# A streaming attention decode on one core: the first load split in 16 and 112 rows, and the semaphores cleared ahead of the last wait

## The chip, the cores and the metric

The kernel runs on one core of a Trainium2 chip. The core has five engines with instruction streams of their own: TensorE (PE in the profile), VectorE (DVE), ScalarE (ACT), GpSimd (POOL) and SyncE (SP), and sixteen DMA engines that move data between the memory (HBM) and the on-chip buffer (SBUF, 128 partitions). The metric is the device time in microseconds (us) of one execution; lower is better. Engines and transfers are kept in order by semaphores: an instruction can wait until a semaphore has reached a value, and an instruction or a transfer adds to one when it is done. A transfer adds 16.

## The reference

Two one-token attention decodes, A and B, with separate inputs, whose outputs are put side by side:

```python
q = (x @ wq).reshape(B, Sq, Hq, Dh)            # x: 1x512, wq: 512x4096, 32 heads of 128
scores = einsum("bhqd,bhkd->bhqk", q, k) * Dh ** -0.5
p = softmax(scores)
o = einsum("bhqk,bhkd->bhqd", p, v)
out = o.reshape(1, 1, 4096) @ wo               # wo: 4096x512
```

A sees the whole cache of 16384 positions, B the last 4096 (a window). Everything is bf16. Each head has its own keys and values, so all of K and V is read once: 128 MiB each for A, 32 MiB each for B, and four weights of 4 MiB. The result has 1024 numbers.

## The kernel before

All large loads are issued by SyncE, one behind the other, and run over all 128 partitions. Three SBUF slots of 8 MiB hold them: slotX and slotY take the key tiles in turn, slotV the values; before the first values arrive, the two halves of slotV hold the weights wq of A and B, and at the end both wo.

There are twenty steps (`steps`), sixteen of A with two heads each and four of B with eight heads each (steps 0, 7, 13 and 19). In each, VectorE multiplies the key tile with the query and adds up along the head's 128 numbers (`scores_prod`, `scores_tree`), TensorE and VectorE find the maximum (`tile_trs`, `tile_max`, `max_all`), ScalarE takes the exponential (`soft`), and TensorE multiplies with the values (`tile_pv`) and folds the result into an accumulator (`tile_fold`). TensorE's part of the loop is a hardware loop.

The order of the loads is written out by hand. Before a first barrier (`tc.close(); tc.compile()`), SyncE issues four loads of 4 MiB without any wait: wq of B (`load_wq`, line 197), the first half of the keys of step 0 (line 181), wq of A, the second half of those keys. ScalarE issues the two small loads of x at the same time. wq goes into slotV by `"(p c) f -> p c f"`: partition p takes four neighbouring rows of the matrix, so 32 KiB in one piece. After that each key load waits until VectorE is done with the slot's earlier tile, and each value load until TensorE is done with slotV. The queue so holds one to two loads ahead of the one that is running.

TensorE starts with the projection of B as soon as its wq is there (line 276), then that of A.

At the end the two wo are loaded, that of B in five pieces (16, 8, 4, 3 and 1 blocks of every partition, line 448), so that little is left to do behind the last piece: sixteen small matmuls (line 595), one copy by VectorE from PSUM into `rows_b` (line 601), and two stores of the result's second half (line 605), one by ScalarE and one by SyncE, that both wait for that copy. The first half of the result was stored by ScalarE before (line 588). All three stores count on one semaphore, `in_out`. GpSimd waits until it has all 48, and then clears all semaphores that the kernel took (`nc.clear_and_free_semaphores(sems)`, line 610): they have to be zero for the next execution.

```python
    wq_in = [None, load_wq(B, wq[1], in_wqB)]
    load_k(0, (0,))
    wq_in[0] = load_wq(A, wq[0], in_wqA)
    load_k(0, (1,))
    tc.close()
    tc.compile()
```

## Time and profile before

| What | Value |
|---|---|
| time, median of 3 runs | 820.95 us (820.79 to 821.01) |
| the profiled execution, its own time | 821.11 us |
| its span, first to last instruction | 819.2 us |
| moved by DMA | 352.40 MB |
| mean rate over the span | 430 GB/s |
| busy: VectorE | 755.7 us (92%) |
| busy: TensorE | 191.5 us (23%) |
| busy: ScalarE | 57.5 us (7%) |
| busy: GpSimd | 3.5 us |

The span is counted from the first to the last instruction of the program; what lies around it, 1.9 us here, is in the execution's time but not in the trace. A core's DMA engines work in packets; a packet of a large load is one partition's piece, 32 or 64 KiB. The chain of waits is followed back from the last instruction and tells what the end waited for. The table of windows gives, for each stretch, the busy time of each engine and then the clock granted to TensorE, the mean share of time in which the sixteen DMA engines were busy, and the rate. Packets are put down there by the time at which they begin, so that in short stretches the share can be over 1.

### The profile page before, as it was taken

To read this page: it belongs to the slowest core of one execution; us is meant where nothing else is said; L and a number is where in the kernel's file an instruction comes from. 1 tells how busy PE (TensorE), PEld (TensorE's weight loads), DVE (VectorE), ACT (ScalarE), POOL (GpSimd) and SP (SyncE) were. 2 spreads that over 40 slices of the span, in tenths; PEclk is the share of its full clock that TensorE was granted. 3 is DMA by queue.
4 is the path that set the end of the run, shared out by engine and by line. 5 is a ranking of instruction groups with operands and counts; after the bars stand their busy time and mean duration, and the time that the engine had idled before them with its cause. 6 is when DMAs were issued, how large, how long until landed. Compare 5 with 4: busy or idle time off the path is not lost. (4 is left out here: it accounts for less than half of the span.)

```text
span 819.2 us, 4049 instructions
## 1 busy us (share of the span) xinstructions
PE 191.5 (23%) x1638; PEld 78.0 (10%) x1638; DVE 755.7 (92%) x264; ACT 57.5 (7%) x165; POOL 3.5 (0%) x15
## 2 busy tenths in 40 slices
PE   3500312213130304030304122131303040303046
PEld 1200101101010101010101011010101010101013
DVE  2899899999999999899999999998999999999992
ACT  0101000001010000100000000010100000000011
POOL 1000000000000000000000000000000000000000
PEclk9765756575665656565656565656656565656567
DMA  9999999999999999999999999999999999999998
GB/s 384 435 435 435 458 413 455 416 454 413 451 419 451 410 432 448 413 458 413 454 416 454 416 454 413 458 413 432 438 454 416 451 416 454 416 434 437 416 432 338
DMA packets 8084, 352.40 MB, mean 430 GB/s; under 512 B 907, under 2 KB 1038, under 8 KB 1294
## 3 DMA queue, kind: packets, MB, share of 16 engines
q1 hardware_dynamic: 8068, 352.33, 99.5%
q8 instruction: 3, 0.05, 0.0%
q14 instruction: 3, 0.02, 0.0%
q10 hardware_dynamic: 10, 0.00, 0.0%
HBM read 352.32 MB, written 0.00 MB: 430 GB/s over the span
## 5 line engine op out<-in xcount | busy, mean ns | idle before, releaser
L306 DVE TENSOR_TENSOR slotX<-slotX,qA 128x16384 bf16<-128x16384 bf16 x18 | 156.3, 8682 | 15.1 <-DMA slotX<-in_A_k_cache_dram 15.1
L315 DVE TENSOR_TENSOR slotY<-slotY 128x8192 bf16<-128x8192 bf16 (+4 forms) x52 | 168.2, 3234 | 1.7
L315 DVE TENSOR_TENSOR slotX<-slotX 128x8192 bf16<-128x8192 bf16 (+4 forms) x44 | 167.0, 3795 | 1.5
L398 PE MATMUL o<-slotV,pm 128*32 128x512 bf16 x1216 | 107.9, 533 | 193.8 <-PEq L165 193.8
L306 DVE TENSOR_TENSOR slotY<-slotY,qA 128x16384 bf16<-128x16384 bf16 x14 | 121.5, 8682 | 8.2 <-DMA slotY<-in_A_k_cache_dram 8.2
L398 PEld LDWEIGHTS o<-slotV,pm 128*32 128x32 bf16 x1216 | 45.1, 128 | 248.8 <-issue 240.7
L391 PE MATMUL sm<-identf,m 128*2 128x128 f32 x20 | 7.4, 372 | 199.5 <-PEq L165 199.5
L306 DVE TENSOR_TENSOR slotY<-slotY,qB 128x16384 bf16<-128x16384 bf16 x6 | 52.1, 8682 | 0.0
L393 PE MATMUL sm<-identf,Mr 2*128 2x2 f32 x20 | 4.7, 233 | 190.2 <-PEq L165 190.2
L354 ACT ACTIVATE bias<-sm 128x1 f32<-128x1 f32 (+1 forms) x20 | 3.4, 171 | 441.8 <-PE sm L393 441.8
L385 ACT COPY osb<-o 128x512 f32<-128x512 f32 x20 | 11.7, 586 | 270.0 <-PE o L398 270.0
L306 DVE TENSOR_TENSOR slotX<-slotX,qB 128x16384 bf16<-128x16384 bf16 x2 | 17.4, 8686 | 12.9 <-ACT qB L282 12.9
L408 PE MATMUL accA<-osb,fwA 128*128 128x512 f32 x38 | 20.8, 630 | 14.8 <-PEq L165 14.8
L322 DVE TENSOR_REDUCE sc<-slotY 128x256 f32<-128x2048 bf16 (+1 forms) x13 | 23.3, 1794 | 0.4
L322 DVE TENSOR_REDUCE sc<-slotX 128x256 f32<-128x2048 bf16 (+1 forms) x11 | 23.0, 2092 | 0.4
L393 PEld LDWEIGHTS sm<-identf,Mr 2*128 2x128 f32 x20 | 3.5, 177 | 196.1 <-issue 196.1
L391 PEld LDWEIGHTS sm<-identf,m 128*2 128x2 f32 x20 | 1.6, 80 | 215.1 <-issue 215.1
L408 PE MATMUL accB<-osb,fwB 128*128 128x512 f32 x40 | 20.5, 594 | 0.5 <-PEq L165 0.5
L367 ACT ACTIVATE pm<-osb,maskA 128x256 bf16<-128x256 bf16 x32 | 14.5, 500 | 0.5
L359 ACT ACTIVATE osb<-sc,bias 128x256 bf16<-128x256 f32 (+1 forms) x24 | 11.3, 470 | 0.6
L276 PE MATMUL t<-slotV,slotY 128*128 128x512 bf16 x32 | 10.0, 488 | 5.0 <-DMA slotV<-in_B_wq_dram 5.0
L276 PE MATMUL t<-slotV,osb 128*128 128x512 bf16 x32 | 8.8, 445 | 9.0 <-DMA slotV<-in_A_wq_dram 9.0
(72 smaller groups left out, 99.4 us busy)
## 6 DMA issues: line engine op xcount, KB each, us to landing
slotV<-in_B_v_cache_dram SPq DMA_DIRECT2D x6, 4096.0 KB, 30.7
slotY<-in_B_k_cache_dram SPq DMA_DIRECT2D x6, 4096.0 KB, 35.3
slotX<-in_B_k_cache_dram SPq DMA_DIRECT2D x2, 4096.0 KB, 30.6
slotX<-in_B_v_cache_dram SPq DMA_DIRECT2D x2, 4096.0 KB, 35.4
slotV<-in_B_wq_dram SPq DMA_DIRECT2D x1, 4096.0 KB, 12.3
slotV<-in_A_wq_dram SPq DMA_DIRECT2D x1, 4096.0 KB, 30.6
slotV<-in_A_wo_dram SPq DMA_DIRECT2D x1, 4096.0 KB, 22.5
slotV<-in_B_wo_dram SPq DMA_DIRECT2D x1, 2048.0 KB, 27.0
```

The lines of the kernel that those rows point to most:

```text
L276: mm = nc.tensor.matmul(qp, lhsT=s.xb[:, j, c, :], rhs=w[:, c, j, g : g + 4, :], start=(k == 0), stop=(k == KC * s.nh - 1),)
L306: return dve.did(nc.vector.tensor_tensor(out=kt, in0=kt, in1=s.q[:, j : j + 1, :].broadcast_to([P, CH, DH]), op=ALU.mult))
L315: t = dve.did(nc.vector.tensor_tensor(out=k[:, :, 0:w], in0=k[:, :, 0:w], in1=k[:, :, w : 2 * w], op=ALU.add))
L322: kfree[T] = dve.did(nc.vector.tensor_reduce(out=sc[:, lo:hi], in_=k[:, :, 0:8], axis=AX.X, op=ALU.add))
L354: t = act.did(nc.scalar.activation(out=bias[:, 0:U], in_=sm[:, P : P + U], func=ACT.Copy))
L359: exped[T] = act.did(nc.scalar.activation(out=p[:, u * n : (u + 1) * n], in_=sc[:, u * n : (u + 1) * n], func=ACT.Exp, scale=inv, bias=bia ...
L367: mm = nc.scalar.activation(out=by_chunk[j], in_=p.rearrange("p (u i c) -> p u i c", u=2, c=4), func=ACT.Copy, scale=s.mask[:, j : j + 1],)
L385: nc.scalar.copy(osb[:, :], o[:, :]).then_inc(to_f, 1)
L391: pe.did(nc.tensor.transpose(sm[0:2, 0:P], m[:, 0:2], identf[:, :]))
L393: pe.did(nc.tensor.transpose(sm[:, P : P + 2], Mr[0:2, :], identf[0:2, 0:2]))
L398: mm = nc.tensor.matmul(o[r0 : r0 + QR, :], lhsT=pm[:, QR * i : QR * (i + 1)], rhs=vf[:, 512 * i : 512 * (i + 1)], start=(i < NG), stop=(i ...
L408: mm = nc.tensor.matmul(a[:, :], lhsT=fw[k][:, :], rhs=osb[:, :], start=False, stop=len(sides) == 1, skip_group_check=True,)
```

## The change

Two places are changed.

The load of B's wq, the first large load of the program, becomes two transfers: partitions 0 to 15, and then partitions 16 to 127. Both count on `in_wqB`, and the projection waits for both (32 in place of 16). All other loads stay as they are; the wq of A keeps one transfer.

At the end a new semaphore, `at_end`, which is not among those cleared, takes the place of the others: VectorE's last copy adds 1 to it, each of the two last stores waits for that and adds 16, GpSimd too waits for the copy alone, clears the semaphores, and adds 1. SyncE waits until `at_end` has 1 + 16 + 16 + 1 = 34 and sets it back to zero. GpSimd's wait for the store of the first half is set right behind that store's issue.

```diff
-    sems = []
+    sems, at_end = [], nc.alloc_semaphore("at_end")
...
-    def load_wq(s, dst, loads):
-        return loads.put(
-            early(nc.sync.dma_start(
-                out=dst.rearrange("p (c f) -> p c f", c=KC), in_=s.wq.rearrange("(p c) f -> p c f", c=KC)
-            ))
-        )
+    def load_wq(s, dst, loads, rows=(P,)):
+        dst, src = dst.rearrange("p (c f) -> p c f", c=KC), s.wq.rearrange("(p c) f -> p c f", c=KC)
+        p0 = 0
+        for n in rows:
+            t = loads.put(early(nc.sync.dma_start(out=dst[p0 : p0 + n, :, :], in_=src[p0 : p0 + n, :, :])))
+            p0 += n
+        return t
...
-    wq_in = [None, load_wq(B, wq[1], in_wqB)]
+    wq_in = [None, load_wq(B, wq[1], in_wqB, (16, P - 16))]
...
-    in_out.put(nc.scalar.dma_start(out=out[0, :, 0:DN], in_=row_a[0:1, :]))
+    pool.need(in_out.put(nc.scalar.dma_start(out=out[0, :, 0:DN], in_=row_a[0:1, :])))
...
-    t = dve.did(nc.vector.tensor_copy(rows_b, last[:, 0:w]))
-    for k, lane in enumerate((act, sp)):
+    nc.vector.tensor_copy(rows_b, last[:, 0:w]).then_inc(at_end, 1)
+    for k, engine in enumerate((nc.scalar, nc.sync)):
         row = QR * (2 * k + 1)
-        lane.need(t)
-        stored = in_out.put(lane.engine.dma_start(
+        engine.wait_ge(at_end, 1)
+        engine.dma_start(
             out=out[0, 0, DN + 2 * k * w : DN + 2 * (k + 1) * w].rearrange("(g f) -> g f", g=2),
             in_=rows_b[row - 1 : row + 1, :],
-        ))
-    pool.need(stored)
+        ).then_inc(at_end, 16)
+    nc.gpsimd.wait_ge(at_end, 1)
     nc.clear_and_free_semaphores(sems)
+    nc.gpsimd.sem_inc(at_end, 1)
+    nc.sync.wait_ge(at_end, 34).then_inc(at_end, -34)
```

## The prediction, made before the result was known

> **What bounds the kernel now.** I read the page first, for the bound:

> ```profile
> span 819.2 us, 4049 instructions
> ...
> DMA  9999999999999999999999999999999999999998
> ...
> DMA packets 8084, 352.40 MB, mean 430 GB/s; under 512 B 907, under 2 KB 1038, under 8 KB 1294
> ...
> q1 hardware_dynamic: 8068, 352.33, 99.5%
> ...
> slotV<-in_B_wq_dram SPq DMA_DIRECT2D x1, 4096.0 KB, 12.3
> ```

> The DMA engines are busy in every slice, SyncE's queue (q1) alone for 99.5% of the span. VectorE's 92% comes second. So the time is: when the stream begins, 352.33 MB at the stream's rate, and what follows the last byte. The packet records of the trace say what the rate is: every DMA engine takes 1.213 us for each 32 KiB piece, 27.0 GB/s, one behind the other with no gap (16 engines give 432 GB/s). It is the same for wq, keys, values and wo. Each 128-row load is 8 pieces to an engine.

> Then the start, in the table of windows (the last two columns are DMA share and GB/s):

> ```profile
> 1.00:1.50 0.50, 0.00 (x0) 0.00 (x0) 0.00 (x0) 0.00 (x0) 0.00 (x0) 1.00 0.00 0
> 1.50:2.00 0.50, 0.00 (x0) 0.00 (x0) 0.00 (x0) 0.00 (x0) 0.00 (x0) 1.00 2.15 524
> 2.00:2.50 0.50, 0.00 (x0) 0.00 (x0) 0.00 (x0) 0.00 (x0) 0.00 (x0) 1.00 1.30 395
> 2.50:3.00 0.50, 0.00 (x0) 0.00 (x0) 0.00 (x0) 0.00 (x0) 0.00 (x0) 1.00 0.36 131
> 3.00:3.50 0.50, 0.00 (x0) 0.00 (x0) 0.00 (x0) 0.00 (x0) 0.00 (x0) 1.00 0.00 0
> 3.50:4.00 0.50, 0.00 (x0) 0.00 (x0) 0.00 (x0) 0.00 (x0) 0.00 (x0) 1.00 1.53 655
> ```

> and in order of time, the issues that go with it:

> ```profile
> 0.74 0.41 SPq L197 DMA_DIRECT2D slotV<-in_B_wq_dram  x1
> 1.20 0.62 SPq L181 DMA_DIRECT2D slotX<-in_B_k_cache_dram  x1
> ```

> The first load is issued at 0.74. Its first sixteen packets, one to an engine, begin between 1.778 and 2.741 (packet records), and nothing new begins until they end, between 3.74 and 4.26, at 3.96 in the mean. They take 1.4 to 2.3 us, 1.9 in the mean, where every later one takes 1.213. From there the stream never stops.

> Last the end, from the chain of waits and the order of time:

> ```profile
> 786.30 30.19 DMA slotV<-in_B_wo_dram
> 816.50 0.04 issue
> 816.54 0.66 PE last L595 x14
> 817.20 0.02 issue
> 817.23 0.29 DVE slotY L601
> ```

> ```profile
> 817.54 0.33 SPq L605 DMA_DIRECT2D out_dram<-slotY  x1
> 817.55 0.26 ACTq L605 DMA_DIRECT2D out_dram<-slotY  x1
> ```

> The last piece of wo is what ends. Behind it stand 0.7 us of matmuls, 0.3 us of copy, and 1.62 us from the stores' issue to the last instruction. The semaphore records split that: the stores' packets move at 818.30, their last increment arrives at 818.833, GpSimd's drain begins at 818.857 (0.10 us), its clearing of the semaphores at 818.986 (0.18 us), and that is the span's end, 819.168.

> **The change part by part.** *The end.* GpSimd's wait, drain and clearing move from behind the stores' landing to behind VectorE's copy, done at about 817.52. Drain, clearing and one increment are 0.10 + 0.03 + 0.18 and some 0.05: done by about 817.95. What hides them is the flight of the stores until 818.833, 0.9 us of cover; were it gone, the 0.31 us would be back. Behind the landing stands SyncE's one wait (semaphore waits in the first barrier are 17 ns long and come 40 to 50 ns after their release). So the last instruction ends near 818.89 in place of 819.17: 0.28 us less. Bounds: 0, if what lies around the span waits for something else, and 0.31, all of drain and clearing. SyncE has nothing queued behind its new wait. GpSimd's added wait for the first half's store (last increment at 815.16) is over 2 us before the copy; nobody waits for GpSimd there. The stores' own waits are the same, on another semaphore: nothing.

> *The start, one issue more.* SyncE issues five transfers ahead of the barrier where it issued four: one more of 0.41 to 0.62 us. The keys' issue slips from 1.20 to about 1.7, still far ahead of its turn at about 12 us. The barrier opens at 3.6 to 4.0 now, behind SyncE's last issue, and would open 0.5 us later; behind it are the constants, the x loads' transposition (now at 7.8, waiting for x) and the projection (now at 13.1, waiting for wq). VectorE's spreading of x ends at 10.9, 2 us ahead of its use: hidden. The next SyncE wait, at 23.1, comes with three loads in flight, so the queue doesn't run dry, and a shift of the stream shifts everything alike.

> *The start, when the stream begins.* A two-row store needs 0.755 us from issue (817.545) to first packet (818.300); the 128-row load needs 1.04 (0.737 to 1.778). Sixteen rows stand near the small one: 0.755 + 0.285 x 14/126 = 0.79, so first packets at about 1.52, 0.25 us earlier. Bounds: 0, since the first packets end together whatever their start, as if all wait for the memory; and 1.2 (0.25 plus the 0.96 us over which engines begin). The engine that lands last at the end isn't the one that began last: increments of wq's load spread over 0.48 us, those of the last wo piece over 1.89, where three engines lag by about 1.6; they fell behind between 80 and 100, 138 and 158, and 544 and 563 us, not at the start.

> [...] No run here shows such a transfer; the trace shows only that 128 partitions get 430 GB/s.

> *The other 112 rows.* Seven pieces to an engine, 7 x 1.213 = 8.49 us, if each engine again has a way of its own. If an engine takes seven neighbouring rows, the groups no longer fall on eights, ways are used by two engines at times: up to 2 x 8.49, so 0 to 8.5 us more. By the nearest row, the 128-row load with no such sharing, I take 0.

> *Sum.* +2.75 at the start, -0.28 at the end: +2.47. The profiled execution's 821.11 (span 819.2 and 1.9 around it) would become 823.58; it stands 0.16 us above the median of 820.95, and against that the forecast is 823.4 us.

> **The rivals.** *Ways are no limit* (an engine's 27.0 GB/s is its own). Then the split only starts the stream earlier: 0.25 and 0.28 less, 820.4; by the bounds 819.4 to 821.0. For it: the same 1.213 us for pieces from four different tensors, which an engine's own rate explains best. Against: one to one of engines and partition groups explains it as well. It decides if the sixteen first packets end before 4.24 in the mean (now 3.96, plus the 0.28 won at the end): up to there the kernel is not slower. This is the case on the other side.

> *The 112 rows share as well.* Groups of seven across groups of eight: I sized it by a share of two for two of seven pieces, 2.4 us more, 825.8; if engines that fall behind then write into others' ways, twice that, 828.3. For it: 112 isn't 128, and nothing in the trace shows the engines' choice of rows there. Against: engines whose neighbour waits could get the full rate.

> *Faster by more than the stream's start explains.* That needs 1.64 us or more less, over the 1.2 + 0.31 of all bounds.

> *The change doesn't do what it says.* If the end is set by another engine's last instruction, 0.28 is lost; this moves each case by that only.

> **How the numbers follow.** A measurement of this kernel can tell about 0.2% from no change, 1.64 us: below 819.3 is faster, above 822.6 slower. Chances: sixteen rows share, 112 don't, 823.4, 0.38; both share, 0.26; no sharing, 820.4, 0.34; the rest 0.02. I put sharing first because a one to one of engines and partitions is given up in just this transfer; a share of four gives 823.4 and is over 822.6, a share of three (1.2 us less) would be within. Slower is so 0.64, same 0.34, faster 0.02. The likeliest case's own range is 822.8 to 824.7 (2.1 to 4.0 at the start). The range of all cases leaves out a tenth on each side: from 820.2, inside the case without sharing, to 827.5, inside the one with both.

> **What would show it.** In the profile of after: the first-load issue in two lines, 16 rows near 0.74 and 112 rows behind it; if I am right, the windows from 2 to 6 us show a rate near a quarter of 430, wq's landing comes 3 us later than 12.6, and the projection starts near 16 in place of 13.1. All stages behind it are shifted by the same, with gaps nowhere. If the 112 rows share, the projection starts at 18 or later. If nothing is shared, the projection starts at or before 13.1 and the span is under 819.2. The span's end should follow the stores' issue by 1.35 us, not 1.63. I am wrong in the sum if the shift at the projection isn't the shift at the end, for then the stream has slack that I don't see; and wrong in the mechanism if first packets end before 4.3.

## The result and the profile after

The change made the kernel slower: 828.61 us (828.43 to 828.98, 6 runs) against 821.01 us (820.79 to 821.05, 6 runs), a ratio of 1.0093 (95% interval 1.008 to 1.0106), or 7.6 us. The profiled execution took 828.75 us, with a span of 827.3 us. The direction was forecast, the size was not: 823.4 us, with a range up to 827.5.

The page of the changed kernel; the row of rates has one figure for each of forty slices of the span, and the first of them was 384 before:

```profile
span 827.3 us, 4052 instructions
...
GB/s 220 415 442 436 452 418 450 412 453 412 450 437 425 426 439 447 414 455 415 447 440 425 444 418 429 433 450 421 440 447 421 447 415 450 418 444 440 417 434 339
DMA packets 8100, 352.40 MB, mean 426 GB/s; under 512 B 923, under 2 KB 1054, under 8 KB 1310
...
q1 hardware_dynamic: 8084, 352.33, 99.5%
...
slotV<-in_B_wq_dram SPq DMA_DIRECT2D x1, 3584.0 KB, 21.1
```

The DMA engines are as busy as before and move the same bytes; the slice that is missing rate is the first. The transfer of the 112 rows needs 21.1 us to land where the whole of wq needed 12.3. In the table of windows (the last two columns are DMA share and GB/s):

```profile
1.50:2.00 0.50, 0.00 (x0) 0.00 (x0) 0.00 (x0) 0.00 (x0) 0.00 (x0) 1.00 6.69 920
2.00:2.50 0.50, 0.00 (x0) 0.00 (x0) 0.00 (x0) 0.00 (x0) 0.00 (x0) 1.00 0.98 131
2.50:3.00 0.50, 0.00 (x0) 0.00 (x0) 0.00 (x0) 0.00 (x0) 0.00 (x0) 1.00 0.00 0
...
8.00:10.00 2.00, 0.00 (x0) 0.00 (x0) 1.97 (x5) 0.00 (x0) 1.80 (x1) 1.00 1.11 262
10.00:12.00 2.00, 0.00 (x0) 0.00 (x0) 0.70 (x5) 0.00 (x0) 0.00 (x0) 1.00 0.92 262
12.00:14.00 2.00, 0.00 (x0) 0.00 (x0) 0.00 (x0) 0.00 (x0) 0.00 (x0) 1.00 0.87 262
```

One of the same rows before:

```profile
10.00:12.00 2.00, 0.00 (x0) 0.00 (x0) 0.89 (x6) 0.00 (x0) 0.00 (x0) 1.00 0.99 426
```

All sixteen first packets begin between 1.5 and 2.5 us (the packet records say 1.760 to 2.103, where before the last one began at 2.741), and then nothing new begins until 5.2 us. That is the transfer of sixteen rows: its packets take 3.83 us in the mean and end at 5.20 to 6.06, where the first packets of before ended at 3.74 to 4.26. Behind them the engines are busy without a break (share near 1) and yet move 262 GB/s. That is the transfer of 112 rows: the first of its seven packets to an engine takes 2.63 to 3.04 us and each of the others 1.65 to 2.37, in place of 1.213. The first packets of the third load are still slow (1.43 to 1.89); from the second on they take 1.213 again.

In order of time, the issues and the projection that waits for wq:

```profile
0.74 0.85 SPq L199 DMA_DIRECT2D slotV<-in_B_wq_dram  x2
...
1.64 0.61 SPq L181 DMA_DIRECT2D slotX<-in_B_k_cache_dram  x1
...
22.30 2.31 PE L277 MATMUL t<-slotV,slotY 128*128 128x512 bf16 x5 [14.39 <-DMA slotV<-in_B_wq_dram]
```

and TensorE before:

```profile
13.10 9.99 PE L276 MATMUL t<-slotV,slotY 128*128 128x512 bf16 x32 [5.01 <-DMA slotV<-in_B_wq_dram]
...
32.49 8.84 PE L276 MATMUL t<-slotV,osb 128*128 128x512 bf16 x32 [8.97 <-DMA slotV<-in_A_wq_dram]
```

The projection starts at 22.30 where it started at 13.10, 9.20 us later. The chain of waits ends as before, only later:

```profile
794.15 30.78 DMA slotV<-in_B_wo_dram
824.93 0.04 issue
824.97 0.66 PE last L596 x10
```

The last matmuls start 8.43 us later (816.54 before). That is less than the 9.20 of the projection, because both wait for the last of a load's sixteen increments, and how far these lie apart is not the same: by 1.38 us for wq of B now and 0.48 before, by 1.8 for the last pieces of wo now and 1.89 before. In the mean of the sixteen increments (semaphore records) wq of B came 8.66 us later and the last pieces of wo 8.6. So what was lost by the start was still missing at the end: the stream gave nothing back.

At the end itself the change does what it says. The stores are issued at 825.977 and SyncE's wait ends at 827.294, 1.32 us later (1.62 before); GpSimd's clearing (826.18 to 826.36 in the trace's records) lies under the stores' flight.

### The profile page after: what moved, and what is told of

It reads as the page before. It is cut to its first block, busy times and chain, and to the rows that moved or that the text cites. A ratio compares the mean times of both kernels' runs of the same rounds, so it can differ in the third digit from the quotient of the medians.

```text
span 827.3 us, 4052 instructions
## 1 busy us (share of the span) xinstructions
PE 189.4 (23%) x1638; PEld 77.2 (9%) x1638; DVE 755.9 (91%) x264; ACT 57.5 (7%) x165; POOL 3.5 (0%) x15
## 2 busy tenths in 40 slices
DMA  9999999999999999999999999999999999999998
DMA packets 8100, 352.40 MB, mean 426 GB/s; under 512 B 923, under 2 KB 1054, under 8 KB 1310
## 3 DMA queue, kind: packets, MB, share of 16 engines
q1 hardware_dynamic: 8084, 352.33, 99.5%
## 6 DMA issues: line engine op xcount, KB each, us to landing
slotV<-in_B_v_cache_dram SPq DMA_DIRECT2D x6, 4096.0 KB, 30.6
slotY<-in_B_k_cache_dram SPq DMA_DIRECT2D x6, 4096.0 KB, 35.3
slotX<-in_B_k_cache_dram SPq DMA_DIRECT2D x2, 4096.0 KB, 39.3
slotX<-in_B_v_cache_dram SPq DMA_DIRECT2D x2, 4096.0 KB, 35.4
slotV<-in_A_wq_dram SPq DMA_DIRECT2D x1, 4096.0 KB, 39.2
slotV<-in_A_wo_dram SPq DMA_DIRECT2D x1, 4096.0 KB, 23.1
slotV<-in_B_wq_dram SPq DMA_DIRECT2D x1, 3584.0 KB, 21.1
```

## The experiments

Theory, formed from these lines: what is lost is lost in the two transfers by rows, because engines write into each other's groups of partitions, the sixteen rows four to a group (the prediction's pick; 3.83 us for a packet is 3.2 times 1.213), the 112 rows seven neighbours to an engine. Rivals: that a small first transfer, or one transfer more, spoils the start of the stream; that neighbouring rows are slow to read from the memory; that the new end has a part in it. Unless another base is named, each kernel is the kernel before with one edit, and is compared with that kernel on the same chip.

### Each part alone

The new end without the split:

```diff
-    wq_in = [None, load_wq(B, wq[1], in_wqB, (16, P - 16))]
+    wq_in = [None, load_wq(B, wq[1], in_wqB)]
```

(against the changed kernel)

> The new end alone, the first load in one transfer as before. Working theory (the split costs all, the end wins its 0.3 us): 820.7 us, 0.3 below before; the last instruction 1.32 us behind the stores' issue, as in the changed kernel, not 1.62. Rival (the end has a cost that the span does not show): at or above 821.0 us.

Measured: 820.1 us against 821.03, a ratio of 0.9989 (0.998 to 0.9998), 0.93 us less. The stores' issue and the span of this kernel:

```profile
817.46 0.33 SPq L606 DMA_DIRECT2D out_dram<-slotY  x1
```

```profile
core 0: 818.8 us, clock 0.610
```

That is below both expectations. From issue to end it is 1.32 us in place of 1.62, the 0.3 us that were worked out; the whole span is 0.41 us shorter in the mean of the runs. The other 0.53 us aren't in the span at all: the time around it is 1.38 us in the mean of 11 runs, and 1.91 in the 21 runs of the kernel before beside them. That is taken up below.

The split without the new end:

```diff
-    wq_in = [None, load_wq(B, wq[1], in_wqB)]
+    wq_in = [None, load_wq(B, wq[1], in_wqB, (16, P - 16))]
```

> The split of the first load alone, the end as before. Working theory: 828.9 us, 0.3 above the changed kernel, with the first sixteen packets at 4 us each and those of the 112 rows near 2 us each. Rival (the loss needs both parts): below 825 us.

Measured: 829.6 us against 821.03, a ratio of 1.0104 (1.0089 to 1.012), 8.57 us more. 8.57 less 0.93 is 7.64, and the whole change measured 7.60: the parts add up, and the split is all of the loss. The sixteen packets take 3.6 us in the mean, those of the 112 rows 1.7 to 3.1.

### Is it the start, or a second transfer?

The same load in two transfers, cut along the rows' length:

```diff
+        for n in cols:
+            t = loads.put(early(nc.sync.dma_start(out=dst[:, c0 : c0 + n], in_=src[:, c0 : c0 + n])))
+            c0 += n
...
-    wq_in = [None, load_wq(B, wq[1], in_wqB)]
+    wq_in = [None, load_wq(B, wq[1], in_wqB, (2048, KC * HQ * DH - 2048))]
```

> The first load in two transfers as well, but cut along the row: all 128 partitions with 4 KiB of each row first, then the other 28 KiB. Theory of partition groups (a DMA engine is slowed where it writes into the partitions of another): each engine keeps its own partitions, so no loss, 820.8 to 821.2 us, and the packets of the second part at full rate. Rival theory of the start (a small first transfer, or one transfer more ahead of the stream, makes the start slow): several us more, 823 to 829 us.

Measured: 821.04 us against 821.03 (ratio 1.0, 0.9991 to 1.0009). One transfer more, and a small one first, costs nothing. It gains nothing either: the first packet begins at 1.766 (1.778 before, 1.760 with the sixteen rows), so in these three kernels how much the first transfer asks for has no part in when the stream begins.

The row split moved to the other wq, third in the queue:

```diff
-    wq_in[0] = load_wq(A, wq[0], in_wqA)
+    wq_in[0] = load_wq(A, wq[0], in_wqA, (16, P - 16))
```

> The same split in 16 and 112 rows, but of the other wq, the third load in the queue; the first load in one transfer. Theory of partition groups: the same loss in another place, 827 to 830 us, with the projection of B at 13.1 us as before and that of A some 8 us late. Rival theory of the start: the stream runs by then, so 821 to 822 us.

Measured: 830.58 us against 821.03, a ratio of 1.0113 (1.0098 to 1.0129). Its TensorE instructions in order of time:

```profile
13.22 8.66 PE L277 MATMUL t<-slotV,slotY 128*128 128x512 bf16 x32 [5.13 <-DMA slotV<-in_B_wq_dram]
...
42.85 9.20 PE L277 MATMUL t<-slotV,osb 128*128 128x512 bf16 x32 [20.53 <-DMA slotV<-in_A_wq_dram]
```

The projection of B is where it was, that of A at 42.85 in place of 32.49. The loss goes with the split, not with the start. It is 9.55 us here, a little over what was expected and 1 us more than in the first place. There the first packets are slow anyway (1.9 us in the kernel before), and part of the sharing probably lies under that; no run shows it apart.

### The sixteen rows by themselves

Four kernels have one more transfer, second in the queue, into a half of slotY that is free then; nothing reads it. A transfer of all 128 rows gives the measure:

```diff
+    rows = B.wq.rearrange("(p c) f -> p (c f)", c=KC)
+    extra_in = in_extra.put(early(nc.sync.dma_start(out=fY[0:128, half : 2 * half], in_=rows[0:128, :])))
...
-    sp.need(freed_y, A.spread)
+    sp.need(freed_y, A.spread, extra_in)
```

> Before, with one more transfer of all 128 rows in the same place: the measure for the others. Theory: an added transfer over all partitions costs its bytes alone, 4 MiB at 432 GB/s = 9.7 us: 830.6 us. Rival (any added transfer has a price of its own): over 831.5 us.

Measured: 830.8 us (two executions) against 820.97, so 9.83 us for 4 MiB, the stream's own 9.7 and nothing beside it. One row of its table of windows, with the extra transfer in it:

```profile
12.00:18.00 6.00, 5.03 (x12) 1.80 (x13) 0.00 (x0) 0.00 (x0) 0.00 (x0) 1.00 1.01 437
```

Sixteen neighbouring rows to partitions 0 to 15 (`out=fY[0:16, ...], in_=rows[0:16, :]`):

> Before, with one more transfer, second in the queue: sixteen neighbouring rows of wq to partitions 0 to 15 of a free place in slotY (0.5 MiB that nothing reads; at the full rate 1.2 us). Theory of partition groups, four engines to a group: 4 packets' time, about 4.9 us, so 825 to 826 us, packets near 4.9 us each. Rival (the engines' own rate is the limit): 822.2 us, packets of 1.2 us.

Measured: 826.11 us (three executions) against 820.94 (ratio 1.0063, 1.0041 to 1.0086), 5.17 us for 0.5 MiB. The sixteen packets take 3.1 to 4.5 us, 3.77 in the mean and less than the 4.9 expected, but the first packets of the keys behind them are slow too, 2.33 in the mean. Both together, less the 1.21 that the keys' packet takes elsewhere, are 4.9 us, four packets' time. The same row of windows:

```profile
12.00:18.00 6.00, 2.83 (x7) 1.03 (x8) 0.00 (x0) 0.00 (x0) 0.00 (x0) 1.00 1.02 175
```

Rows that lie apart in the memory, to the same partitions (`out=fY[0:16, ...], in_=rows[0:128:8, :]`):

> Sixteen rows of the matrix that lie apart (every eighth of the 128 pieces) to partitions 0 to 15. Theory of partition groups: as with neighbouring rows to these partitions, packets near 4.9 us, 825 to 826 us. Rival (reading neighbouring rows is what is slow): packets of 1.2 to 2.4 us, 822 to 823.5 us.

Measured: 825.96 us (three executions) against 820.94, packets of 2.8 to 4.3 us:

```profile
12.00:18.00 6.00, 4.36 (x13) 1.68 (x14) 0.00 (x0) 0.00 (x0) 0.00 (x0) 1.00 0.99 175
```

The same rate: in both kernels 32 packets of 32 KiB begin in these 6 us, and 80 with the 128-row transfer. Neighbouring rows, to partitions 0, 8, 16 ... 120 (`out=fY[0:128:8, ...], in_=rows[0:16, :]`):

> The same sixteen neighbouring rows of the matrix, but to partitions 0, 8, 16 ... 120. Theory of partition groups, two engines to a group: about 2.4 us, so 823 to 824 us, packets near 2.4 us. Rival (reading neighbouring rows of the memory is what is slow): the same as with neighbouring partitions, packets near 4 to 5 us.

Measured: 823.56 us against 820.94 (ratio 1.0032, 1.002 to 1.0043), 2.62 us. (Eight of the nine executions took 823.3 to 823.7 us. The ninth, whose trace was kept, took 831.15; in it the loads behind run at 1.36 us a packet up to about 80 us, and why is not known.) So it matters where the rows are written, not where they are read: 5.17 and 5.02 us for partitions 0 to 15, from near and from far rows, and 2.62 for the same sixteen rows spread by eights. At 1.21 us for the bytes at full rate these are shares of 4.3, 4.1 and 2.2. A transfer of sixteen rows to sixteen different groups, which would show what such a small transfer costs with no sharing, was not run.

The four and two engines to a group of the expectations fit these shares within a tenth. How many groups there are, and which partitions each of them has, no run shows.

### The 112 rows by themselves

(`out=fY[16:128, ...], in_=rows[16:128, :]`)

> Before, with one more transfer of 112 rows to partitions 16 to 127 (3.5 MiB that nothing reads, at the full rate 8.5 us, so 829.5 us without any loss). Theory of partition groups with seven neighbouring rows to an engine: packets near 2 us in place of 1.2, some 5 to 7 us more, 834 to 837 us. Rival (the 112 rows were slow in the changed kernel only because the sixteen rows before them had put the engines out of step): 829.5 to 831 us.

Measured: 834.96 us (two executions) against 820.94 (ratio 1.0173, 1.0144 to 1.0203): 14.02 us for 3.5 MiB that take 8.49 at full rate, 5.5 us more, with nothing before it that had put the engines out of step:

```profile
18.00:24.00 6.00, 4.84 (x23) 1.99 (x21) 0.00 (x0) 1.17 (x2) 0.00 (x0) 1.00 1.04 262
```

262 GB/s, the rate of the changed kernel's start. 3.96 for the sixteen rows (5.17 - 1.21) and 5.5 for the 112 make 9.5, the 9.55 of the split in the third load. All seven packets of an engine are slow, 1.71, 2.20, 1.81, 1.73, 2.10, 2.22 and 2.10 us in the mean. So the engines hardly take sixteen neighbouring rows at a time, one each: that would be like the transfer to partitions 0 to 15, which came to four packets' time.

If an engine takes seven neighbouring rows, the first packets of the sixteen engines go to partitions 16, 23, 30 ... 121. That pattern alone (`out=fY[16:128:7, ...], in_=rows[0:16, :]`):

> Before, with sixteen more rows, second in the queue, to partitions 16, 23, 30 ... 121: the first of each seven, if an engine of the 112-row transfer takes seven neighbours. Theory of partition groups, each group on its own: fourteen groups, only two of them with two engines, so twelve packets of 1.2 us and four of 2.4, 1.3 to 2.4 us in all, 822.3 to 823.3 us. Rival (a held group holds the others up as well): all packets near 2 us and 823 us or more.

Measured: 823.21 us against 820.97 (ratio 1.0028, 1.0015 to 1.0041), 2.24 us, 1.03 over the bytes. All sixteen packets are slow, 1.49 to 1.98 us, 1.69 in the mean. The first sixteen packets of the 112 rows take 1.44 to 1.98, 1.71 in the mean: the two patterns look alike, as they should if the rows are dealt by sevens. That the chip deals them so is inferred from this; no trace names an engine's rows.

The time of 823.21 fits both expectations; the packets decide. With groups each on its own, twelve of the sixteen were to take 1.2 us, and none did. On every engine this packet and the next, the first of the keys, together take 3.5 to 3.8 us where 2.43 is the rule, about one packet's time more. That a group with two engines holds the other engines up too is inferred: a transfer with no group used twice, which would settle it, was not run, and how it would hold them up stays open.

The inference rests on the expectation's count of groups, which is an estimate: eight partitions to a group, as the 128-row load has eight packets to an engine, make fourteen groups of 112 partitions, and with neighbours in a group two of them, 16 to 23 and 72 to 79, get two of these rows. No run shows such groups. By them the rows spread by eights would each have had a group alone, and those came to 2.2 shares.

### The half microsecond around the span

In the new end without the split, another engine waits for the stores. GpSimd, after its clearing:

```diff
-    nc.gpsimd.sem_inc(at_end, 1)
-    nc.sync.wait_ge(at_end, 34).then_inc(at_end, -34)
+    nc.gpsimd.wait_ge(at_end, 33).then_inc(at_end, -33)
```

> The first load in one transfer, the end as in the changed kernel (GpSimd clears while the stores are on their way) except that GpSimd, not SyncE, waits for the stores after that. The new end alone took 0.93 us off: 0.4 of the span and 0.53 of the time around it (1.91 before, 1.38 with it). Theory that GpSimd being the engine that ends last costs the 0.53 around the span: 820.6 to 820.7 us, 1.9 around it. Rival (clearing semaphores as the last thing costs it): 820.1 us, 1.4 around it.

Measured: 820.77 us against 820.97 (ratio 0.9997, 0.9988 to 1.0006), with 1.94 us around the span in the mean of 11 runs. Its stores' issue and its span:

```profile
817.81 0.33 SPq L606 DMA_DIRECT2D out_dram<-slotY  x1
```

```profile
core 0: 819.1 us, clock 0.618
```

The span still ends 1.33 us behind the issue; only the time around it is back. And ScalarE:

```diff
-    nc.sync.wait_ge(at_end, 34).then_inc(at_end, -34)
+    nc.scalar.wait_ge(at_end, 34).then_inc(at_end, -34)
```

> The same, but ScalarE waits for the stores. Theory that GpSimd alone is slow to end: 820.1 us and 1.4 us around the span, as with SyncE. Rival (SyncE alone is quick to end): 820.6 us, 1.9 around it.

Measured: 820.31 us against 820.97 (ratio 0.9991, 0.9982 to 1.0), 1.54 us around the span, between the two expectations and nearer to the first. So the time around the span goes with the engine that ends last: 1.38 us with SyncE, 1.54 with ScalarE, 1.94 with GpSimd, whether or not it clears anything then. Why GpSimd takes longer lies outside the trace and stays open.

The new end alone, with SyncE waiting, is the fastest kernel of this study: 820.1 us.

## Why the prediction was right and wrong

- **The bound.** Right. The stream of loads is the time: in the mean of the increments wq came 8.66 us later and the last pieces of wo 8.6, and only the end gave something back. The shift at the projection (9.20) was not the shift at the last matmuls (8.43), which the prediction called a sign of slack; the increments show that only the last of the sixteen differed by so much. (The 12.6 us given there for wq's landing is the first increment; the projection waits for the last, at 13.06.)
- **The extra issue, and the work behind the barrier.** Right. The keys' issue slipped to 1.64 (1.7 forecast), VectorE's spreading was done by 10.7, and the projection waited for wq alone. The column split, with the same issues, cost nothing.
- **When the stream begins.** Wrong by 0.25 us. First packets were to begin at 1.52, by interpolating between a two-row store and a 128-row load; they began at 1.760. The difference between those two rows was not one of size, and the lower bound, 0, was the better choice.
- **Where the sixteen rows go.** Right that where the rows are written sets the time, and in its size: four engines to a way was worth 4.85 us, and the transfer by itself took 5.17. No run shows the four engines to a way; from the rows of the case it was only a pick between two ends, so that it came out so well is in part luck. What the runs gave are shares of 4.3 and 4.1. In the changed kernel the first packets ended 1.7 us later and not 2.4 or more, but the packets behind them were slow as well. The split's 8.57 less the 5.5 that the 112 rows cost alone leaves 3.0 for the sixteen rows, where the sum had 2.75.
- **The other 112 rows.** This is the step that failed. "By the nearest row, the 128-row load with no such sharing, I take 0": measured 5.5 us alone, and of the 8.6 us in place only 1.7 were lost when the first sixteen packets ended. With 5.5 in place of 0 and 0.93 in place of 0.28 at the end, the sum is 7.3, and 7.6 was measured. The 128-row load wasn't the nearest row. In it, as the prediction read it, each engine has its own partitions, and whether that is needed was just what was in question. I had named the reason why 112 rows could differ, given bounds of 0 to 8.5, and then taken the end where the reason doesn't hold.
- **The rival that came true**, that both transfers share, had 0.26 and 825.8 to 828.3 us; 828.61 is above it by 0.3. Its sign came true as well: the projection was to start at 18 or later, and started at 22.30. It was priced too low, at two slow pieces of an engine's seven, or twice that; all seven were slow. The argument against it, that "engines whose neighbour waits could get the full rate", didn't hold: with sixteen rows at step seven, none did (1.49 to 1.98 us a packet in place of 1.213).
- **The range.** It left out a tenth on the upper side, inside the rival that came true. Both transfers rest on the same question (does writing into shared groups cost?), so their costs go together: where the sixteen rows share, the 112 were likelier to share than the 0.26 in 0.64 that they were given, and the upper end should have been their sum of 828.3 and more.
- **The end.** Direction right, size a third: 0.28 forecast, 0.93 measured. The part from the stores' issue to the last instruction was right (0.28 forecast, 0.30 measured). The bound of 0.31 was wrong, since it counted only what the trace shows; 0.53 us came off the time around the span, because the engine that ends last was another. The last 0.1 us, in the span ahead of the stores, is within what the runs differ by.
- **No sharing (820.4 us, 0.34).** Refuted by the four transfers of sixteen rows: 5.17, 5.02, 2.62 and 2.24 us, where the bytes alone take 1.21.

## What to carry to other kernels

In a stream like this, split a load along the rows' length, not across partitions: a transfer over all 128 partitions cost its bytes alone, whole (9.83 us for 4 MiB more) or cut along its rows (821.04 us against 821.03), while sixteen partitions ran at about 100 GB/s (0.5 MiB in 5.17 us) and 112 of 128 at 262. In this stream without gaps such a loss stayed to the last byte (8.66 us at wq, 8.6 at the last pieces of wo), so price each transfer of an odd shape by itself, and price two that depend on the same unknown together. And at the end of a kernel, see which engine ends last: moving GpSimd's clearing under the stores and letting SyncE wait was worth 0.9 us, more than half of it outside the trace.

## What the runs showed that was not expected

- 112 of 128 partitions are far from seven eighths of the rate: 262 GB/s against 437, in the changed kernel and in the transfer by itself.
- With sixteen rows at partitions 16, 23 ... 121 all sixteen engines are slow: every packet took 1.49 us or more where 1.213 is the rule. That a group which two engines write into holds up the others is one reading; it rests on an estimated count of groups and is not shown.
- The time around the span, 1.9 us, isn't a constant of the program: 1.38, 1.54 or 1.94 us by the engine that ends last.
- The first packet of the stream began at 1.760 to 1.778 us whether the first transfer had 16 rows, 128 rows of 4 KiB, or 128 rows of 32 KiB.
